# A three-stage mixer on one core: centred rows in place of normalized ones, paired folds and sums, attention state in column halves, and a new hand-written order

## The chip, the cores and the metric

The kernel runs on one core of a Trainium2 chip. The metric is the device time of the core in microseconds (us), as the median of several runs. A profiled execution gives the trace that the rows below come from. Engines: PE is TensorE's matmuls, PEld its weight loads, DVE is VectorE, ACT is ScalarE, POOL is GpSimd, SP is SyncE, which here issues DMAs.

## The reference

```python
def _attn_ref(q, k, v):                       # (2, 8, 768, 64) each, float32
    gamma = 1.0 - 2.0 ** (-5.0 - np.arange(H))
    for t in range(S):
        state = gamma * state + outer(k[:, :, t], v[:, :, t])
        y[:, :, t] = scale * (q[:, :, t] @ state)

def _moe_ref(x, w_ch1, w_ch2):                # x: (2, 768, 512), weights 512x2048, 2048x512 float64
    X = np.fft.fft(np.fft.fft(x, axis=1), axis=2)
    u = x + np.real(X)
    un = (u - mean(u)) / np.sqrt(var(u) + 1e-06)
    return u + np.maximum(un @ w_ch1, 0.0) @ w_ch2

def _moe2_ref(x, w_in, conv_w, w_out):        # weights 512x1024, 3x1024, 1024x512 float64
    h = np.maximum(x @ w_in, 0.0)
    conv_out = three-tap convolution of h along the sequence
    return (h * sigmoid(conv_out)) @ w_out
```

The three run one after the other. Data is float32, weights arrive as float64 and are turned into float32 on the chip.

## The kernel before, in words

Everything is a job, a short Python function that issues a few instructions. A string, ORDER, names the jobs one by one, and each engine gets its instructions in exactly that order; there is no scheduler. Each engine runs its own queue in order and waits at an instruction until its data and its buffers are there. A number such as 7 in a name is one of 12 chunks of 128 tokens, 6 for each of the two batches.

Attention. Lq, Lk, Lv load a chunk's tiles (256 KB each) through SP's queue, V scales v by the decay on POOL (L225), K and Q transpose k and q on PE (L231) with a copy by ACT (L232), S makes the scores of 8 heads in 64-row halves (L244, masked by DVE on L246), A adds the chunk to the running state (L256: per pair of heads one matmul of 128x128, of which only the two diagonal 64x64 blocks are used, copied by ACT on L260), O makes the output from state (L274) and scores (L277), and DVE scales it (L288).

Mixing. F folds a chunk's 512 features to sums and differences on POOL (L306 to L308), G folds again on DVE (L314 to L317, four instructions). After six chunks of a batch b, butterflies b0.0 to b0.9 combine the chunks (DVE, three of them on POOL: L337, L347, L348), t is the transform along the tokens (PE L369 to L373, copied by ACT on L374, L375), p the one along the features (L385 to L394), m and r add it to the residual stream u: m the first half of the tokens by DVE (L418, L419, two L411), r the other half, gathered in reverse by an indirect DMA (rev), by POOL (two L411).

First block. s takes mean and variance (L489, L490), dev the square root on ACT (L494), rec the reciprocal with one Newton step on DVE (L499 to L504, six small instructions for a group of three tiles), n normalizes a tile (L509, DVE), x transposes it (L531) and splits it in a high and a low part (ACT L535, DVE L536). U multiplies by a slice of the first weights, with ReLU on ACT (L560) and its low part on DVE (L561), D multiplies by the second and accumulates in PSUM, Z adds the sum to u (L572). Every product is three fp32r matmuls (high by high, high by low, low by high: L131 to L133). Batch 0 takes the 16 weight slices in three groups, batch 1 in one.

Weights. f fetches half a slice (512 KB), d decodes float64 to float32 on DVE (L465 to L469), e splits into high and low (ACT L459, then DVE or POOL L461).

Second block: y transposes, h the first product (tile hi), c, a, w the convolution, the gate and its split, P the last product (tile po) with a copy and the output DMA.

PSUM has eight banks, handed out in rotation. Batch 0 goes first through attention and mixing; its first block starts with U00.0 while batch 1 is still in attention and mixing, whose transform (t1) then stands between the first D jobs.

Of the kernel before, what the change touches and what calls it, by code (L numbers as in the profile page):

```python
# [16 lines left out]
P = 128  # L17
# [108 lines left out]
def mixer_kernel(ctx, tc, q, k, v, w_ch1, w_ch2, w_in, conv_w, w_out,  # L126
# [174 lines left out]
    def fold1(n):  # L301
# [78 lines left out]
    def dft_features(b, t):  # L380
        pq = pqt[b]

        def cosines(name, lo, rows):
# [3 lines left out]
            nc.tensor.matmul(g[0:rows, 129:257], pq[:, 1, lo:lo + rows], t2[:, 1, 0:P], start=True, stop=True)  # L387
# [6 lines left out]
        nc.tensor.matmul(qs[:, 129:257], pq[:, 3, sl], t2[:, 3, 0:P], start=True, stop=True)  # L394
        ny = cosines(f"ny{b}", HB, 1) if t == 0 else None
        mixes[b, t] = mix = fp.tile([P, 3, 258], F32, tag="h2", name=f"mix{b}{t}", bufs=H2)
        nc.scalar.copy(mix[:, 0, 0:257], qs[:, 0:257])
        products[b, t] = (pc, ny)

    def halves(b, t):  # L400
        w, e, dd = (mixes[b, t][:, i, :] for i in range(3))

        def low(x):
            return x.rearrange("p (j g) -> p j g", j=2)[:, :, 0:P]

        def high(x):
            return x[:, 1:257].rearrange("p (j g) -> p j g", j=2)[:, :, ::-1]

        def acc(eng, x, i, y):
            xv = x[:, t, i * 256:(i + 1) * 256].rearrange("p (g j) -> p j g", j=2)  # L410
            eng.tensor_tensor(xv, xv, y, op=ALU.add)  # L411

        return w, e, dd, low, high, acc

    def mixed(b, t):
        pc, ny = products[b, t]
        w, e, dd, low, high, acc = halves(b, t)
        nc.vector.tensor_tensor(dd[:, 0:257], pc[:, 0:257], w[:, 0:257], op=ALU.subtract)  # L418
        nc.vector.tensor_tensor(e[:, 0:257], pc[:, 0:257], w[:, 0:257], op=ALU.add)  # L419
        acc(nc.vector, u[b][0], 0, low(dd))  # L420
        acc(nc.vector, u[b][0], 1, high(e))
# [84 lines left out]
    def normalized(b, s, t):  # L506
# [64 lines left out]
    def residual(b, s, hi, t):  # L571
        nc.vector.tensor_tensor(u[b][s][:, t, :], u[b][s][:, t, :], accs[b, s, hi, t], op=ALU.add)  # L572
# [161 lines left out]
```

## Time and profile before

| what | value |
|---|---|
| median of 3 runs | 534.2 us (533.27 to 535.11) |
| profiled execution: its time, and the span of its trace | 531.92 us, 530.1 us |
| PE busy | 510.2 us (96%) |
| DVE busy | 337.7 us (64%) |
| ACT busy | 162.4 us (31%) |
| POOL busy | 87.6 us (17%) |
| mean granted TensorE clock | 0.997 |

Busy time counts the instructions of an engine that run, also while one stands in the pipeline behind another; the rest of the span is waiting. Each float32 matmul leaves two records in the trace, a transpose or an fp32r matmul one.

### The profile page before, as it was taken

How to read it: one execution, taken by the hardware profiler on the slowest of the kernel's cores; microseconds unless marked ns; L12 is line 12 of the kernel's file. 1: busy time of each engine (PE TensorE's matmuls, PEld its weight loads, DVE VectorE, ACT ScalarE, POOL GpSimd, SP SyncE). 2: the span in 40 equal slices, each digit the busy share in tenths (PEclk: the TensorE clock that was granted, in tenths of full speed). 3: DMA queues.
4: the chain of work that ended last, by engine and by line, in shares of the span. 5: the costliest groups of instructions: out<-in, count | busy, mean ns of one | idle time of the engine just before them, and what ended most of it. 6: DMA issues, size and time to landing. Idle time of an engine off the chain costs nothing.

```text
span 530.1 us, 7396 instructions
## 1 busy us (share of the span) xinstructions
PE 510.2 (96%) x2968; PEld 460.5 (87%) x2968; DVE 337.7 (64%) x593; ACT 162.4 (31%) x303; POOL 87.6 (17%) x98
## 2 busy tenths in 40 slices
PE   6998897998999999999999999999999999999997
PEld 5897787977998989889988998988999999988886
DVE  1578999999799877865221114887746675756511
ACT  3332344314322222121111112232255664445200
POOL 1545773450132201100000000120000000000000
PEclk9999999998999999999999999999999999999999
DMA  9999540213464043322000000344000000011111
GB/s 192 222 250 272 163 140 0 101 41 120 143 211 130 16 156 120 119 81 41 1 0 1 0 1 0 120 158 160 0 1 1 1 1 0 21 40 41 40 41 59
DMA packets 60807, 42.49 MB, mean 80 GB/s; under 512 B 42083, under 2 KB 54884, under 8 KB 60774
## 3 DMA queue, kind: packets, MB, share of 16 engines
q1 hardware_dynamic: 60294, 40.46, 27.1%
q0 software_dynamic: 480, 1.57, 1.0%
q8 instruction: 23, 0.38, 0.3%
q14 instruction: 10, 0.08, 0.0%
HBM read 37.30 MB, written 4.72 MB: 79 GB/s over the span
## 4 chain that ended last, share of the span: by engine, by line
PE 73%; DVE 12%; DMA 5%; issue 4%; POOL 4%; ACT 1%; SPq 0%; POOLq 0%; DVEq 0%; ACTq 0%
PE ac L133 7%; PE ac L132 7%; PE ac L131 7%; PE h L131 6%; PE h L133 6%; PE h L132 6%; PE po L132 4%; PE hi L133 4%; PE po L131 4%; PE hi L131 4%; PE hi L132 4%; PE po L133 4%; DMA xin<-in_v_dram 2%; DVE word L467 2%; PE px L277 2%
## 5 line engine op out<-in xcount | busy, mean ns | idle before, releaser
L561 DVE SCALAR_TENSOR_TENSOR h<-h,h 128x384 fp32r<-128x384 f32 x64 | 34.5, 552 | 76.8 <-ACT h L560 76.8
L131 PE MATMUL ac<-wt,h 128*128 128x512 f32 x192 | 76.6, 399 | 0.0
L133 PE MATMUL ac<-wt,h 128*128 128x512 f32 x192 | 76.2, 397 | 0.3 <-DVE h L561 0.3
L132 PE MATMUL ac<-wt,h 128*128 128x512 f32 x192 | 75.7, 394 | 0.0
L560 ACT ACTIVATE h<-h 128x384 fp32r<-128x384 f32 x64 | 30.8, 490 | 127.1 <-PE h L133 124.6
L461 POOL TENSOR_TENSOR wt<-word,wt 128x512 fp32r<-128x512 f32 x16 | 21.8, 1360 | 215.5 <-ACT wt L459 215.5
L459 ACT CAST wt<-word 128x512 fp32r<-128x512 f32 x48 | 29.5, 620 | 91.0 <-DVE word L469 88.5
L133 PEld LDWEIGHTS ac<-wt,h 128*128 128x128 f32 x192 | 36.0, 188 | 9.8 <-DVE h L561 1.5
L618 DVE SCALAR_TENSOR_TENSOR cv<-hb,cw,cv 128x768 f32<-128x768 f32 x32 | 32.5, 1018 | 15.5 <-ACT cv L616 14.8
L132 PEld LDWEIGHTS ac<-wt,h 128*128 128x128 f32 x192 | 36.1, 188 | 6.4
L131 PEld LDWEIGHTS ac<-wt,h 128*128 128x128 f32 x192 | 36.1, 188 | 6.2
L132 PE MATMUL po<-wt,g 128*128 128x512 f32 (+1 forms) x104 | 39.2, 377 | 0.0
L131 PE MATMUL po<-wt,g 128*128 128x512 f32 (+1 forms) x104 | 39.2, 377 | 0.0
L133 PE MATMUL po<-wt,g 128*128 128x512 f32 (+1 forms) x104 | 39.1, 376 | 0.0
L467 DVE SCALAR_TENSOR_TENSOR word<-raw,word 128x512 int32<-128x512 int32 x48 | 36.7, 764 | 1.6
L469 DVE SCALAR_TENSOR_TENSOR word<-raw,word 128x512 int32<-128x512 int32 x48 | 36.5, 760 | 1.6
L461 DVE TENSOR_TENSOR wt<-word,wt 128x512 fp32r<-128x512 f32 x32 | 24.0, 749 | 14.7 <-ACT wt L459 14.7
L647 DVE COPY ob<-po 128x512 f32<-128x512 f32 (+1 forms) x13 | 8.4, 648 | 28.3 <-PE po L133 28.3
L465 DVE TENSOR_SCALAR word<-raw 128x512 int32<-128x512 int32 x48 | 22.9, 478 | 3.4 <-POOL wt L461 2.6
L277 PE MATMUL px<-xin,work 128*128 128x64 f32 x192 | 23.8, 274 | 0.9 <-DVE work L246 0.9
L277 PEld LDWEIGHTS px<-xin,work 128*128 128x128 f32 x192 | 22.7, 192 | 1.8 <-DVE work L246 1.6
L133 PEld LDWEIGHTS po<-wt,g 128*128 128x128 f32 x104 | 19.6, 188 | 3.9
(176 smaller groups left out, 1170.4 us busy)
## 6 DMA issues: line engine op xcount, KB each, us to landing
raw<-in_moe_w_ch_dram SPq DMA_DIRECT2D x32, 512.0 KB, 3.7
raw<-in_moe_w_out_dram SPq DMA_DIRECT2D x8, 512.0 KB, 3.4
raw<-in_moe_w_in_dram SPq DMA_DIRECT2D x8, 512.0 KB, 3.4
xin<-in_q_dram SPq DMA_DIRECT2D x12, 256.0 KB, 4.6
xin<-in_k_dram SPq DMA_DIRECT2D x12, 256.0 KB, 5.1
xin<-in_v_dram SPq DMA_DIRECT2D x12, 256.0 KB, 5.0
out_dram<-ob SPq DMA_DIRECT2D x11, 256.0 KB, 2.0
xd<-states SPq DMA_DIRECT2D x6, 256.0 KB, 3.2
```

Of the source, the lines that this page charges most:

```text
L131: nc.tensor.matmul(o, ah, bh, start=start, stop=False)
L132: nc.tensor.matmul(o, ah, bl, start=False, stop=False)
L133: nc.tensor.matmul(o, al, bh, start=False, stop=stop)
L277: nc.tensor.matmul(px[:, h * D:(h + 1) * D], at[:, h, :], v_tile(n)[:, h, :], start=c == 0 and h == 0, stop=h == H - 1, skip_group_check=True)
L459: nc.scalar.copy(wt[:, 0, j], f32(word))
L461: eng.tensor_tensor(wt[:, 1, j], f32(word), f32(wt[:, 0, j]), op=ALU.subtract)
L465: nc.vector.tensor_scalar(word, raw[:, :, 1], 3, 0x3FFFFFF8, op0=ALU.logical_shift_left, op1=ALU.bitwise_and)
L467: nc.vector.scalar_tensor_tensor(word, raw[:, :, 1], -0x40000000, word, op0=ALU.bitwise_and, op1=ALU.bitwise_or)
L469: nc.vector.scalar_tensor_tensor(word, raw[:, :, 0], 29, word, op0=ALU.logical_shift_right, op1=ALU.bitwise_or)
L560: nc.scalar.activation(h2[:, 0], ps[:, :HB], AF.Relu)
L561: nc.vector.scalar_tensor_tensor(h2[:, 1], ps[:, :HB], 0.0, f32(h2[:, 0]), op0=ALU.max, op1=ALU.subtract)
L618: nc.vector.scalar_tensor_tensor(cv, hb[:, j:j + S], f32(cw[:, j * NF2 + f:j * NF2 + f + 1]), cv, op0=ALU.mult, op1=ALU.add)
```

## The change

- **Centred rows.** n only subtracts the mean; the division by the deviation is moved behind the second product, into Z, which multiplies the sum by 1/deviation while it adds it to u (ReLU lets a positive factor through). So x and U no longer need dev and rec, Z does. For 9 of 12 tiles the subtraction is an ACT instruction with the negated mean as bias, and s gets one small DVE instruction for that. The pools of the statistics are four deep in place of two.
- **Folds and mixed sums in pairs.** G is two DVE instructions of 2x128 in place of four; F is two POOL instructions, and two ACT instructions of one column. m is two instructions of 2x129 and one of 512 in place of two and two; r is one POOL instruction in place of two. Some matmuls of p get a 129th column.
- **State by heads in column halves.** A is, per head, one matmul with 64 weight columns and 64 moving columns, in place of one of 128x128 per pair of heads.
- **Work moved.** O's scaling of chunks 0, 6, 7 goes from DVE to ACT in 8 instructions of 64 columns each; V of chunk 5 from POOL to ACT in 8 also; F of chunk 4 and butterflies b0.2 and b1.2 from POOL to DVE. Five decoded words lie in PSUM banks. The identity is loaded from ACT's queue, Lv1 from POOL's.
- **A new job, warm:** three matmuls of 128x512 on zeros into a bank that nobody reads.
- **A new ORDER.** Its first line, of before and of the change, shows the start.

```diff
 ORDER = """
-Lq0 ident clear Q0 Lk0 K0 Lk1 K1 Lv0 masks V0 S0 A0 Lq1 Lk2 Lq2 Lv1 V1 Lk3 Lv3 V3 Q1 Lq3 O0 Lv5 F0 Q2 Lq4 S1 V5 G0 K3
+Lq0 clear Lv0 Lv3 ident masks V0 V3 Q0 Lk0 K0 A0 Lv1 S0 V1 Lq1 Lk1 K1 Lq2 Lk4 Lk2 Lv2 V2 Lk3 Lv4 Q1 Q2 Lq4 Lq3 f2 f0
...
+PX_ACT = (0, 6, 7)
+V_ACT = (5,)
+FOLD_DVE = (4,)
+FLY_DVE = ((0, 2), (1, 2))
+LOW_POOL = (0, 3, 6, 9, 12, 15, 18, 21, 24, 27, 30, 33, 36, 39, 40, 42)
+WORD_BANK = (2, 8, 22, 37, 38)
+CENTRE_ACT = ((0, 0, 0), (0, 0, 1), (0, 0, 2), (0, 1, 0), (1, 0, 1), (1, 0, 2), (1, 1, 0), (1, 1, 1), (1, 1, 2))
+WARM = (512, 512, 512)
...
+    def start_clock():
+        ps = bank("idle")
+        z = sbd[0].rearrange("p a e -> p (a e)")
+        for n in WARM:
+            nc.tensor.matmul(ps[:, 0:n], z[:, 0:P], z[:, 0:n], start=True, stop=True)
...
         for hp in range(NP):
-            nc.tensor.matmul(st[:, hp * P:(hp + 1) * P], pair(k_tile(n), hp), pair(v_tile(n), hp),
+            for j in range(2):
+                lo = hp * P + j * D
+                nc.tensor.matmul(st[j * D:(j + 1) * D, lo:lo + D], k_tile(n)[:, 2 * hp + j, :], v_tile(n)[:, 2 * hp + j, :],
...
-        nc.vector.tensor_tensor(o[:, 0:129], e[:, 0:129], e[:, 256:127:-1], op=ALU.add)
-        nc.vector.tensor_tensor(o[:, 129:256], od[:, 1:128], od[:, 255:128:-1], op=ALU.subtract)
-        nc.vector.tensor_tensor(o[:, 256:384], e[:, 0:128], e[:, 256:128:-1], op=ALU.subtract)
-        nc.vector.tensor_tensor(o[:, 384:512], od[:, 1:129], od[:, 255:127:-1], op=ALU.add)
+        o2 = o.rearrange("p (k n) -> p k n", k=4)
+        nc.vector.tensor_tensor(o2[:, 2:0:-1, :], eod2[:, :, 0:P], eod2[:, :, 256:P:-1], op=ALU.subtract)
+        nc.vector.tensor_tensor(o2[:, 0:4:3, :], two(0, 259), two(129, 257)[:, :, ::-1], op=ALU.add)
...
-        nc.vector.tensor_scalar(un, u[b][s][:, t, :], mv[:, t, 0:1], ve[:, 2, t:t + 1],
-                                op0=ALU.subtract, op1=ALU.mult)
+        if (b, s, t) in CENTRE_ACT:
+            nc.scalar.activation(un, u[b][s][:, t, :], AF.Identity, bias=ve[:, 4, t:t + 1])
+        else:
+            nc.vector.tensor_scalar(un, u[b][s][:, t, :], mv[:, t, 0:1], None, op0=ALU.subtract)
...
-        nc.vector.tensor_tensor(u[b][s][:, t, :], u[b][s][:, t, :], accs[b, s, hi, t], op=ALU.add)
+        nc.vector.scalar_tensor_tensor(u[b][s][:, t, :], accs[b, s, hi, t], norm[b, s][1][:, 2, t:t + 1], u[b][s][:, t, :],
+                                       op0=ALU.mult, op1=ALU.add)
```

Three places of the order follow, as the built programs have it. First PE's queue early in attention (pk, pq: transposes; px: O's matmuls; st: the state; idle: the bank of warm). Before, from K3 to O1:

```order
L231 MATMUL pk_192<-ident,xin_77 128x128 x4
L256 MATMUL st_129<-xin_80,xin_79 128x128 x4
L231 MATMUL pq_210<-ident,xin_80 128x128 x4
L274 MATMUL px_217<-states,work_82 128x128 x4
L277 MATMUL px_217<-xin_80,work_82 128x64 x8
```

With the change, from K2 to the second state update:

```order
L244 MATMUL pk_207<-ident,xin_77 128x128 x4
L289 MATMUL px_213<-states,work_82 128x128 x4
L292 MATMUL px_213<-xin_80,work_82 128x64 x8
L222 MATMUL idle<-states 128x512 x3
L271 MATMUL st_112<-xin_80,xin_79 64x64 x8
```

The state takes eight matmuls in place of four, and warm stands between O1 and it.

Second, ACT's queue ahead of batch 0's transform along the tokens (g is t's bank, pq its result). Before, the last rows ahead of t0.4's copies and those copies:

```order
L232 COPY work_83<-pq_576 128x512
L232 COPY work_83<-pk_610 128x512
L459 CAST wt_569<-word_459 128x512
L374 COPY pq_618<-g_619 1x6x64
L375 COPY pq_618<-g_619 1x1
```

With the change:

```order
L301 ACTIVATE u_72<-px_633,decay 128x64 x8
L301 ACTIVATE u_72<-px_661,decay 128x64 x8
L245 COPY work_82<-pq_682 128x512
L323 ACTIVATE eod<-u_72 128x1
L324 ACTIVATE eod<-eod 128x1
L396 COPY pq_696<-g_697 1x6x64
L397 COPY pq_696<-g_697 1x1
```

The scaling of O6 and O7, 16 instructions, and the single columns of F7 now stand ahead of the copies of t.

Third, what stands ahead of the first tile that x transposes. Before, on DVE (ve: the deviations; un: the normalized tile):

```order
L246 TENSOR_TENSOR work_83<-sc_824,mask 128x4x128
L499 TENSOR_SCALAR ve_713<-mv_712 128x3
L500 RECIPROCAL ve_713<-ve_713 128x3
L501 TENSOR_TENSOR ve_713<-ve_713 128x3
L502 TENSOR_TENSOR ve_713<-ve_713 128x3
L503 TENSOR_SCALAR ve_713<-ve_713 128x3
L504 TENSOR_TENSOR ve_713<-ve_713 128x3
L509 TENSOR_SCALAR un_849<-u_70,mv_712,ve_713 128x512
```

With the change, on ACT, between the copies of p:

```order
L419 COPY mix_768<-qs_765 128x258
L447 COPY mix_759<-ny_755 1x2x129
L448 COPY mix_759<-ny_755 1x2x129
L541 ACTIVATE un_781<-u_70,ve_776 128x512
L419 COPY mix_790<-qs_787 128x258
```

The tile un no longer stands behind the six small instructions, and it is on another engine.

## Rows read from the trace of the kernel before

**Rows 1.** Busy time of each engine in four stretches (start:end, length, busy us, records).

```profile
4.17:98.10 93.93, 84.59 (x751) 76.77 (x752) 73.96 (x139) 33.34 (x70) 49.58 (x59) 1.00 0.73 176
98.10:121.30 23.20, 20.49 (x111) 18.33 (x110) 22.88 (x42) 4.70 (x9) 11.21 (x11) 1.00 0.18 58
121.30:160.00 38.70, 38.70 (x216) 34.86 (x217) 33.74 (x58) 13.73 (x29) 8.58 (x8) 0.96 0.54 170
160.00:526.00 366.00, 365.72 (x1891) 329.97 (x1890) 206.65 (x355) 109.31 (x194) 17.08 (x15) 1.00 0.15 48
```

**Rows 2.** Whom PE waited for, whole span: us in total, times, longest.

```profile
PE pq L231 <- DMA ident<-in_c_ident_dram: 4.2, 1, 4.2
PE g L369 <- issue: 2.3, 1, 2.3
PE tr L531 <- DVE un L509: 2.2, 2, 1.7
PE g L369 <- DVE fold L351: 1.9, 1, 1.9
PE pq L231 <- DMA xin<-in_q_dram: 1.3, 1, 1.3
...
PE st L256 <- POOL xin L225: 0.9, 1, 0.9
...
PE h L132 <- DVE un01l L536: 0.8, 1, 0.8
```

**Rows 3.** Stretches of 2 us around t1's start; the granted clock is the third last.

```profile
120.00:122.00 2.00, 0.73 (x8) 0.61 (x9) 1.93 (x4) 0.00 (x0) 0.00 (x0) 0.92 0.00 0
122.00:124.00 2.00, 2.00 (x10) 1.31 (x9) 1.28 (x3) 1.05 (x3) 0.00 (x0) 0.50 0.01 1
124.00:126.00 2.00, 2.00 (x15) 2.00 (x15) 1.93 (x4) 1.37 (x4) 0.00 (x0) 0.72 0.80 239
```

**Rows 4.** Timeline, the first centred tile's chain of before.

```profile
84.22 1.28 ACT L494 ACT_TABLE_LOAD   x1
...
87.92 1.00 DVE L509 TENSOR_SCALAR un<-u,mv,ve 128x512 f32<-128x512 f32 x2
...
89.07 0.63 PE L531 MATMUL tr<-ident,un 128*128 128x128 f32 x4 [1.73 <-DVE un L509]
```

**Rows 5.** Groups of DVE instructions, whole span: busy us, mean ns of one.

```profile
L314 DVE TENSOR_TENSOR fold<-eod 128x129 f32<-128x129 f32 x12 | 6.6, 551 | 3.6 <-POOL eod L307 3.5
...
L315 DVE TENSOR_TENSOR fold<-eod 128x127 f32<-128x127 f32 x12 | 5.3, 439 | 0.0
L317 DVE TENSOR_TENSOR fold<-eod 128x128 f32<-128x128 f32 x12 | 4.4, 367 | 0.0
...
L316 DVE TENSOR_TENSOR fold<-eod 128x128 f32<-128x128 f32 x12 | 3.4, 280 | 0.0
...
L418 DVE TENSOR_TENSOR mix<-pc,mix 128x257 f32<-128x257 f32 x6 | 2.5, 410 | 0.0
```

**Rows 6.** Timeline, attention: start, length, instruction.

```profile
14.89 0.97 PEld L244 LDWEIGHTS sc<-work 64*128 64x128 f32 x16 [0.17 <-issue]
...
16.47 1.06 PE L256 MATMUL st<-xin,xin 128*128 128x128 f32 x8
...
31.70 1.87 PEld L277 LDWEIGHTS px<-xin,work 128*128 128x128 f32 x16
```

**Rows 7.** Timeline, the start: first scores, and a load's issue on SP's queue.

```profile
8.02 2.08 PE L244 MATMUL sc<-work 64*128 64x128 f32 x16
...
8.23 1.07 SPq L191 DMA_DIRECT2D xin<-in_v_dram  x1
```

**Rows 8.** Groups of ACT instructions, whole span.

```profile
L374 ACT COPY pq<-g 128x384 f32<-128x384 f32 x8 | 7.1, 892 | 3.2 <-PE g L373 3.2
...
L375 ACT COPY pq<-g 128x1 f32<-128x1 f32 x8 | 1.9, 233 | 0.0
...
L630 ACT CAST g<-cv 128x128 fp32r<-128x128 f32 x4 | 1.2, 299 | 0.0
```

More of the change, by code (lines that the diff above doesn't have):

```diff
@@ L206, in clear @@
     def clear():
+        nc.vector.memset(sbd[0], 0.0)
+        nc.gpsimd.memset(sbd[1], 0.0)
         nc.vector.memset(eps, EPS)
-        for i in range(2):
-            nc.gpsimd.memset(sbd[i], 0.0)
+    def start_clock():
[3 more added lines that the diff above has]
+            nc.tensor.matmul(ps[:, 0:n], z[:, 0:P], z[:, 0:n], start=True, stop=True)
     xdram = {}
@@ L386, in cosines @@
             nc.tensor.matmul(g[0:rows, 0:129], pq[0:1, 4, lo:lo + rows], alt, start=False, stop=True)
-            nc.tensor.matmul(g[0:rows, 129:257], pq[:, 1, lo:lo + rows], t2[:, 1, 0:P], start=True, stop=True)
+            nc.tensor.matmul(g[0:rows, 129:258], pq[:, 1, lo:lo + rows], t2[:, 1, :], start=True, stop=True)
             return g
@@ L398, in dft_features @@
+        nc.scalar.copy(mix[:, 0:258], qs[:, 0:258])
         products[b, t] = (pc, ny)
     def halves(b, t):
[L401 to L411, printed above, removed]
@@ L413, in halves, with runs, two_runs, features @@
-        return w, e, dd, low, high, acc
+        m = mixes[b, t]
+        def runs(lo, n):
+            return m[:, lo:lo + 2 * n].rearrange("p (j g) -> p j g", j=2)[:, :, 0:P + 1]
+        return runs(0, P + 1), runs(258, P + 2), runs(518, P + 1)[:, :, ::-1], m[:, 258:778].rearrange("p (i s) -> p i s", i=2)
+    def two_runs(x):
+        return x[:, 0:258].rearrange("p (j g) -> p j g", j=2)
+    def features(x):
+        return x.rearrange("p (i g j) -> p i j g", i=2, j=2)
     def mixed(b, t):
@@ L416, in mixed @@
         pc, ny = products[b, t]
[L417 to L421, printed above, removed]
+        w, dd, e, both = halves(b, t)
+        nc.vector.tensor_tensor(dd, two_runs(pc), w, op=ALU.subtract)
+        nc.vector.tensor_tensor(e, two_runs(pc), w, op=ALU.add)
@@ L422, in mixed @@
+        x = features(u[b][0][:, t, :])
+        nc.vector.tensor_tensor(x, x, both.rearrange("p i (j g) -> p i j g", j=2)[:, :, :, 0:P], op=ALU.add)
         if t == 0:
-            nc.scalar.copy(e[0:1, 0:257], ny[0:1, 0:257])
-            nc.scalar.copy(dd[0:1, 0:257], ny[0:1, 0:257])
+            nc.scalar.copy(e[0:1], two_runs(ny)[0:1])
+            nc.scalar.copy(dd[0:1], two_runs(ny)[0:1])
     def mixed_back(b, t):
-        w, e, dd, low, high, acc = halves(b, t)
+        both = halves(b, t)[3]
@@ L428, in mixed_back @@
         eng = nc.vector if (b, t) in BACK_DVE else nc.gpsimd
-        acc(eng, u[b][1], 0, low(e))
-        acc(eng, u[b][1], 1, high(dd))
+        x = features(u[b][1][:, t, :])[:, ::-1]
+        eng.tensor_tensor(x, x, both[:, :, 1:259].rearrange("p i (j g) -> p i j g", j=2)[:, :, :, P - 1::-1], op=ALU.add)
     chunks = {}
@@ L450, in decode @@
         i, j = divmod(h, 2)
-        words[h] = word = fp.tile([P, 512], I32, tag="word", name=f"word{i}{j}", bufs=2)
+        if h in WORD_BANK:
+            words[h] = word = psum.tile([P, 512], I32, tag="ps", name=f"word{i}{j}")
+        else:
+            words[h] = word = fp.tile([P, 512], I32, tag="word", name=f"word{i}{j}", bufs=2)
         to_float32(word, raws[h])
@@ L680, in mixer_kernel @@
                 jobs[f"s{b}{s}.{t}"] = later(moments, b, s, t)
-                jobs[f"n{b}{s}.{t}"] = later(normalized, b, s, t)
+                jobs[f"n{b}{s}.{t}"] = later(centred, b, s, t)
                 jobs[f"x{b}{s}.{t}"] = later(norm_transposed, b, s, t)
```

98 lines of the change are left out of this document (52 added, 46 removed).

## The prediction

> **What bounds the kernel now.** I read the four stretches first [rows 1]. From 121.3 us to 526 PE is busy 404.4 of 404.7 us, with fp32r products back to back: nothing that DVE, ACT or POOL saves there shortens anything, since PE has no wait to give up. What can be won lies ahead of that, where two stretches wait. From PE's first matmul at 4.17 to U00.0 at 98.1 PE is busy 84.59 of 93.93 us, so 9.3 us are waits; from 98.1 to 121.3 it is busy 20.49 of 23.20, so 2.7 are. The other engine to look at is DVE: 74.0 of 93.9 in the first of these, but 22.88 of 23.20 in the second. There DVE is full, and PE waits for it.
>
> Second, whom PE waits for [rows 2]. The first wait (4.2 us, for the identity and the first q) is the head, which stays, as the first q sets it too. Of the rest, four are named by the change: 2.2 us in two waits of x's transposes for un, 2.3 us of t0's first matmul (its butterflies are the last of a DVE and POOL chain, although the row names no engine), 1.9 us of t1's first matmul for the last butterfly of batch 1, and 0.9 and 0.8 us for V and for the low part of a tile. 1.3 us is for a load.
>
> Third, the clock [rows 3]. After the 1.9 us wait, which ends at 121.27, the granted clock is 0.92, 0.50 and 0.72 in three stretches of 2 us, so near 1.2 GHz in the middle one, and 1.00 again after. Lost are (0.08 + 0.50 + 0.28) times 2 us, 1.7 us, within busy time that no wait shows. So t1's wait costs 3.6 us, not 1.9.
>
> All that could be won from waits and clock is then 9.3 + 2.7 + 1.7 = 13.7 us, 2.6% of the time.
>
> **The change part by part.** The sum is made against the profiled execution, 531.92 us; the median of the runs, 534.2, is 2.3 above it, and I add that at the end.
>
> *Centred rows.* Before, x's first transpose waits 1.73 us for un, which DVE ends after ACT has loaded the table for the square root (1.28 us, from 84.22) and after the six small instructions of rec [rows 4]. Now un needs only the mean; it stands on ACT among the copies of p, before the table is loaded at all. Both waits for un can go: **-2.2 us**. Bounds 0 and -2.2: 0 if something else is then late at that place, such as the scores of chunk 10, which DVE masks there. Z now needs dev and rec, but Z comes four D jobs after U00.0, and stays one DVE instruction on the same two tiles; I price that at nothing. The cover is those D jobs; without it Z would pay the old 2.2 us.
>
> *Pairs on DVE.* The four instructions of G take 551 + 439 + 367 + 280 ns on average, 1.64 us; where POOL is quiet each takes what the L316 row shows, 0.28, so 1.12 [rows 5]. The two that replace them have 256 columns each, like the 257 of L418, 0.41: 0.82 us. A chunk saves 0.3 to 0.8 us, twelve chunks 3.6 to 9.8; I take 6, as half of the L314 mean is waiting on POOL's side. The three scalings and four subtractions that go to ACT are set against F4, b0.2, b1.2 and a memset that come to DVE, and the merged mixed sums are a small gain on top. So DVE does 6 to 8 us less before t1 out of 97 [rows 1]. This isn't time by itself; it is what shortens the waits for DVE: t0's 2.3 us, t1's 1.9 with its 1.7 of clock, and the two small ones.
>  - t0: the butterflies of batch 0 also wait for POOL, whose part of that chain stays but for b0.2. I take half, **-1.1** (bounds 0, -2.3).
>  - t1: between U00.0 and t1 the same six U and three D jobs stand as before, so PE's cover is the same, and DVE has the last of the four-instruction folds and POOL's three folds out of that stretch. The lead wanted is 1.9 us of 22.9. I take all, **-3.6** (bounds 0, -3.6).
>  - V10 and the low part: half of 1.7, **-0.8**.
>
> *State in column halves.* Before, eight records of a state update take about 1 us: each is held by a weight load of 128 columns, about 0.12 us. With 64 columns there are 16 records. Two rows bound them [rows 6]. The output matmuls (L277) move 64 columns on weights of 128 and pass 16 records in 1.87: +0.8 to +0.9 us for each of ten updates, +8.5 in all. The score matmuls, in alternating 64-row halves, pass 16 records of 128 columns in 0.97, half the pace of the undivided ones, so halves run side by side there; if column halves do the same with half the columns, 16 take 0.5, -0.5 each, -4.9 in all. Half of the columns to load and half to move, one after the other, is 16 times 0.055, 0.88: **-0.9** over ten. I take that, being between.
>
> *Warm.* Three float32 matmuls of 512 columns. A state update before moves 4 times 128 columns in about 1 us [rows 6], so each costs that: 2.9 us of PE. Nothing hides it at its place, for PE has hardly a wait there; but some of the waits after it, 1.3 us for a q tile among them, are for loads that come no later for it. I take half, **+1.3** (bounds 0, +2.9). It comes too late for the start, where the first scores take 2.08 us [rows 7] against about 1 later [rows 6].
>
> *The start.* K0's load now stands behind q, two v, the mask and the decay on SP's queue, where it stood behind q and the identity; loads follow each other at about 1.1 us [rows 7], so K0 is 2 to 3 us later. V0, S0 and A0 needed the decay and v anyway, which come earlier now. **+0.5** (0 to +2.5).
>
> *ACT ahead of t0.* The scaling of O7 is now eight ACT instructions of 64 columns: between 233 ns for one column and 299 for 128 [rows 8], 0.25 each, so 2.1 us, and two single columns of F7 another 0.5. They stand in ACT's queue right before the first of t0's five pairs of copies (0.89 + 0.23 us a pair). PE's t jobs are slower than a pair by some tenths and p begins with what is copied first, which catches up part of 2.6: **+1.0** (0 to +2.6).
>
> *At nothing:* Z by deviation, the columns 129, words in PSUM, the identity's queue, r in one instruction. They are behind a full PE or on engines with room (ACT 33 of 94 us, POOL 50 of 94 in the first stretch [rows 1]).
>
> Sum: -2.2 - 1.1 - 3.6 - 0.8 - 0.9 + 1.3 + 0.5 + 1.0 = -5.8. 531.92 - 5.8 = 526.1, and with the 2.3 between the profiled execution and the median, **528.4 us**, 1.1% faster.
>
> **The rivals.**
> 1. *Column halves at the price of the L277 rows.* Eight matmuls held by their loads cost +8.5 in place of -0.9: -5.8 + 9.4 = +3.6, **537.8 us**, slower. Against it: the weights are half as wide here. For it: where a queue goes from undivided to row halves, the score's first load shows 0.17 us of idle with nothing waited for [rows 6]; two such changes for each of ten updates would add up to 3.4 us, 541.2 with both. The Trainium skill ("TensorEngine Tiling (Array Packing)", Key Properties) says that a change of tiling mode drains TensorE; no run here yet shows it for column halves. It decides from 1.6 us for an update, against 1.0 before: there the other terms are used up.
> 2. *Waits move, they don't go.* The loads set the pace until about 50 us, DVE's place at t1 is taken by two decoded halves and butterfly b1.2, and PE waits for those. Then -2.2, -1.1 and -3.6 shrink to a third (-2.3), and the additions stay: -2.3 - 0.4 - 0.9 + 2.8 = -0.8, **533.4 us**, no difference. For it speaks that DVE is 99% busy before t1 and the first long DVE chains are unchanged.
> 3. *More than forecast.* Halves side by side (-4.9 in place of -0.9) and all waits named gone (-1.2 - 0.8 more), warm hidden (-1.3): -5.8 - 7.3 = -13.1, **521.1 us**.
>
> **How the numbers follow.** A measurement of this kernel can hardly tell 0.3%, 1.6 us, from no change. Forecast (524 to 531.5): 0.55. Rival 3 (518 to 524): 0.15. Rival 2 (within 1.6 us of 534.2): 0.13. Rival 1 and other losses, such as a start later by the full 2.5 us with warm unhidden: 0.17. So faster 0.70, same 0.13, slower 0.17. The range goes from near rival 3's own time, 520, to 535.5, just over rival 2; it leaves out the deepest part of rival 3 and most of rival 1, together below 2 in 10.
>
> **What would show it.** U00.0 starts near 94 us in place of 98.1, with no wait of tr for un. The first matmul of t1 waits less than 0.5 us and the granted clock stays at 1.00 there. A state update's 16 records take 0.8 to 1.0 us; 1.6 or more is rival 1, 0.5 rival 3. G takes near 0.8 us on DVE. After t1 PE is as full as before, and the stretch from t1 to the end is as long. The forecast is wrong if state updates are slow, if U00.0 starts at 98 or later, or if the new order puts a wait of PE behind 121 us, where there was none: there any wait costs its full length.

## The result, and the profile after

The changed kernel takes 528.83 us (median of 4 runs, 528.11 to 530.10), the kernel before beside it 534.65 (533.27 to 536.80): a ratio of 0.989, 95% interval 0.9851 to 0.9929. It is 1.1% faster. The profiled execution took 528.11 us, with a span of 526.3 against 530.1.

First the stretches of the changed kernel that answer to [rows 1]: up to U00.0, from there to t1's first matmul, the next 39 us, the rest. Behind them stand four stretches of 2 us around U00.0, and a stretch that comes up later; the granted clock is the third last number.

```profile
4.42:97.75 93.33, 83.69 (x838) 73.51 (x838) 66.60 (x120) 45.41 (x129) 48.17 (x48) 0.98 0.74 168
97.75:119.37 21.62, 21.58 (x107) 19.94 (x108) 18.48 (x33) 5.22 (x12) 4.42 (x4) 0.92 0.36 116
119.37:158.10 38.73, 38.73 (x222) 34.70 (x222) 32.87 (x60) 13.28 (x29) 6.81 (x6) 1.00 0.43 136
158.10:525.00 366.90, 364.66 (x1890) 330.06 (x1888) 205.72 (x352) 112.05 (x198) 18.39 (x14) 1.00 0.16 50
...
94.00:96.00 2.00, 0.89 (x4) 0.89 (x5) 1.86 (x7) 1.06 (x2) 0.35 (x1) 0.60 0.00 0
96.00:98.00 2.00, 1.32 (x7) 0.92 (x5) 1.13 (x3) 1.47 (x3) 2.00 (x3) 0.50 0.76 254
98.00:100.00 2.00, 1.96 (x6) 1.56 (x7) 2.00 (x5) 0.41 (x3) 0.30 (x1) 0.50 0.56 184
100.00:102.00 2.00, 2.00 (x10) 2.00 (x9) 1.16 (x4) 0.07 (x1) 0.76 (x1) 0.70 1.03 386
...
20.00:26.00 6.00, 6.00 (x60) 3.82 (x61) 4.74 (x8) 3.03 (x9) 1.71 (x2) 1.00 1.06 262
```

Second, whom PE waits for over the whole span; this answers to [rows 2].

```profile
PE pq L244 <- DMA xin<-in_q_dram: 4.4, 1, 4.4
PE sc L257 <- ACT work L245: 3.3, 4, 1.2
PE pk L244 <- DMA xin<-in_k_dram: 2.8, 1, 2.8
PE tr L564 <- ACT un L541: 2.0, 1, 2.0
PE h L136 <- ACT un00h L568: 0.7, 1, 0.7
PE st L271 <- ACT states L275: 0.4, 1, 0.4
```

Third, rows of the timeline, in order of time: warm, a state update, t0's start, ACT and PE ahead of U00.0, and the work around t1's start.

```profile
8.30 1.11 PE L244 MATMUL pk<-ident,xin 128*128 128x128 f32 x4 [2.79 <-DMA xin<-in_k_dram]
...
19.82 2.79 PE L222 MATMUL idle<-states 128*128 128x512 f32 x6
...
22.54 0.55 PEld L271 LDWEIGHTS st<-xin,xin 128*64 128x64 f32 x16 [0.76 <-issue]
22.54 0.69 PE L271 MATMUL st<-xin,xin 128*64 128x64 f32 x16
...
59.92 1.75 ACT L301 ACTIVATE u<-px,decay 128x64 f32<-128x64 f32 x8 [0.94 <-PE px L292]
60.25 0.27 PE L391 MATMUL g<-tabs,fold 128*1 128x65 f32 x2
...
92.38 1.28 ACT L524 ACT_TABLE_LOAD   x1
93.67 0.30 ACT L524 ACTIVATE ve<-mv,eps 128x3 f32<-128x3 f32 x1
93.87 0.56 ACT L568 CAST un01h<-tr 128x512 fp32r<-128x512 f32 x1
94.34 0.72 ACT L541 ACTIVATE un<-u,ve 128x512 f32<-128x512 f32 x1
95.11 1.97 PE L564 MATMUL tr<-ident,un 128*128 128x128 f32 x8 [1.97 <-ACT un L541]
97.75 0.69 PE L136 MATMUL h<-un00h,wt 128*128 128x384 f32 x1 [0.68 <-ACT un00h L568]
...
109.26 1.29 POOL L369 TENSOR_TENSOR fold<-fold,fold 128x512 f32<-128x512 f32 x1 [6.73 <-DVE fold L361]
...
117.29 0.69 DVE L373 TENSOR_TENSOR fold<-fold 128x512 f32<-128x512 f32 x1
119.37 0.33 PE L391 MATMUL g<-tabs,fold 128*128 128x65 f32 x2
```

What to see. t0 and t1 start without a wait, where 2.3 and 1.9 us stood before [rows 2]; t1's last butterfly ends at 117.98, 1.4 us early, where it was 1.9 us late. A state update passes its 16 records in 0.69 us, where eight took 1.06 [rows 6]. But the first matmul of U00.0 stands at 97.75, hardly ahead of 98.1. The wait for un is still there: 2.0 us, now for ACT, and 0.7 behind it. Tile n00.1, the centring of the first block's second tile, stands in ACT's queue behind two things of the other half of the tokens: its square root (dev01), whose table takes 1.28 us to load, and the split of its tile x01.0 (un01h). And the clock that was lost at t1 before [rows 3] is lost here. Counted in PE's busy time alone, since a low clock costs nothing while PE waits anyway, the four stretches lose 0.40 x 0.89 + 0.50 x 1.32 + 0.50 x 1.96 + 0.30 x 2.00, 2.6 us, against 1.6 by the same count from [rows 3].

Up to U00.0 the waits as a whole did not shrink: PE waits 9.6 us of the first stretch, where it was 9.3 [rows 1]. Two kinds grew. Scores wait 3.3 us in four places for ACT's copies of transposes, where it was 0.7 in one, and K's load costs 2.8 in place of 0.8. ACT is busy 45.4 us there in place of 33.3; whether that is what holds up the scores was not tried.

By stretch, the 3.8 us between the two spans are: 0.25 lost in the head, 0.6 won up to U00.0, 1.6 from there to t1, 1.9 behind t1's start, of which 1.7 is the clock that fell there before. The 2.2 us of the last stretch in which PE is not busy are the tail behind its last matmul, which ends near 522.9.

### The profile page after: what moved, and what is told of

The parts are those of the page before. It is cut to its first block, busy times and chain, and to the rows that moved or that the text cites. A ratio compares the mean times of both kernels' runs of the same rounds, so it can differ in the third digit from the quotient of the medians.

```text
span 526.3 us, 7589 instructions
## 1 busy us (share of the span) xinstructions
PE 508.7 (97%) x3054; PEld 458.2 (87%) x3054; DVE 324.2 (62%) x565; ACT 177.2 (34%) x368; POOL 78.5 (15%) x75
## 4 chain that ended last, share of the span: by engine, by line
PE 76%; DVE 6%; issue 6%; POOL 5%; ACT 3%; DMA 2%; SPq 1%; POOLq 0%
PE h L138 7%; PE h L136 7%; PE h L137 7%; PE ac L138 7%; PE ac L137 6%; PE ac L136 6%; PE hi L138 4%; PE hi L137 4%; PE hi L136 4%; PE po L136 4%; PE po L138 4%; PE po L137 4%; PE px L292 3%; PE sc L257 2%; PE tr L564 2%
## 5 line engine op out<-in xcount | busy, mean ns | idle before, releaser
L488 POOL TENSOR_TENSOR wt<-word,wt 128x512 fp32r<-128x512 f32 x16 | 21.2, 1323 | 224.5 <-ACT wt L486 214.1
L496 DVE SCALAR_TENSOR_TENSOR word<-raw,word 128x512 int32<-128x512 int32 x48 | 37.4, 779 | 1.6
L494 DVE SCALAR_TENSOR_TENSOR word<-raw,word 128x512 int32<-128x512 int32 x48 | 34.2, 712 | 1.6
L488 DVE TENSOR_TENSOR wt<-word,wt 128x512 fp32r<-128x512 f32 x32 | 22.0, 689 | 13.7 <-ACT wt L486 13.7
L492 DVE TENSOR_SCALAR word<-raw 128x512 int32<-128x512 int32 x48 | 24.3, 506 | 3.7 <-POOL wt L488 2.6
L259 DVE TENSOR_TENSOR work<-sc,mask 128x512 f32<-128x512 f32 x24 | 15.4, 684 | 17.0 <-PE sc L257 16.9
L136 PE MATMUL h<-un00h,wt 128*128 128x384 f32 x64 | 22.4, 350 | 0.7 <-ACT un00h L568 0.7
```

Of the source, the lines that this page charges most:

```text
L136: nc.tensor.matmul(o, ah, bh, start=start, stop=False)
L488: eng.tensor_tensor(wt[:, 1, j], f32(word), f32(wt[:, 0, j]), op=ALU.subtract)
L492: nc.vector.tensor_scalar(word, raw[:, :, 1], 3, 0x3FFFFFF8, op0=ALU.logical_shift_left, op1=ALU.bitwise_and)
L494: nc.vector.scalar_tensor_tensor(word, raw[:, :, 1], -0x40000000, word, op0=ALU.bitwise_and, op1=ALU.bitwise_or)
L496: nc.vector.scalar_tensor_tensor(word, raw[:, :, 0], 29, word, op0=ALU.logical_shift_right, op1=ALU.bitwise_or)
```

## The experiments

Each kernel was timed in five rounds against the kernel before; "ratio" is to that kernel. Unless said otherwise an experiment starts from the changed kernel. They ran in three groups, and medians are best compared within a group: the first four, the next four, the last four.

**The changed kernel once more (a0_again).** No edit.

> The changed kernel once more, beside the others of this call on the same chip: ratio to before 0.989 as on record, about 528.8 us. It gives the ground that the others are measured from, and a second profile: if the 2.0 us wait for the centred tile and the clock of 0.5 after it are the work of the order and not of one execution, they stand there again.

527.90 us, ratio 0.9888 (0.9859 to 0.9918), with the same 2.0 us wait of tr, the same fall of the clock there, and t1 at 119.09. This is what the others of its group stand against.

**The second root later (e1_root_later).** dev01 and rec01 moved behind U00.0's tiles:

```diff
-... F11 s01.1 dev01 rec01 O10 x01.0 n00.1 ... U01.1 f7 d7 e7 t1.0 dev00 rec00 t1.2 ...
+... F11 s01.1 O10 x01.0 n00.1 ... U01.1 f7 d7 e7 t1.0 dev00 rec00 dev01 rec01 t1.2 ...
```

> dev01 and rec01 (ACT's table load, 1.28 us, and root, 0.30) move from ahead of the centred tile n00.1 to behind rec00; nothing else. Theory A (the wait that centring was to remove came back because dev01 stands ahead of n00.1 in ACT's queue): un starts where x01.0's transposes free its buffer, at about 93.2 in place of 94.34, so the wait of 1.97 us falls to 0.8, the clock falls for a shorter time, and the kernel is 1 to 4 us faster than the changed one (525 to 528). Theory B (U00.0 is held by the DVE and PE work of chunks 10 and 11): U00.0 stays at 97.7 and the time within 0.5 us of the changed kernel.

528.41 us, ratio 0.9889 (0.9863 to 0.9915): no gain, where theory A had 1 to 4 us. At its place the edit did a part of what was meant: tr waits 1.3 us in place of 2.0, the clock stays at 1.00, U00.0 starts at 96.77 and t1 at 117.27, 1.8 us sooner than in a0_again.

```profile
94.95 1.09 PE L564 MATMUL tr<-ident,un 128*128 128x128 f32 x8 [1.30 <-ACT un L541]
```

So the root accounts for 0.7 of the 2.0 us. In the 1.3 that stay, n00.1 still stands behind x01.0, the other half's tile: ACT splits that at 93.69 and centres n00.1 at 94.17. Then PE waits 1.5 us for a weight slice (L488) near 130 and 0.5 us for DVE's h, where there was no wait.

**The first block's tiles first (e7_block_first).** On top of that, n00.1 ahead of the other half's tiles:

```diff
-x00.0 n01.0 s01.2 ... s01.1 O10 x01.0 n00.1 x00.1 x00.2 n01.1 n01.2 ... b1.5 x01.1 ...
+x00.0 n00.1 s01.2 ... s01.1 O10 x00.1 x00.2 n01.0 n01.1 ... b1.5 x01.0 n01.2 x01.1 ...
```

> As e1, and the three tiles of U00.0 are centred and transposed before any tile of the other half (n00.1 takes the place of n01.0, x01.0 stands behind U00.1). Theory A: no wait of tr for un, the granted clock stays at 1.00, U00.0 starts 3 us earlier and runs at full rate: 4 to 6 us faster than the changed kernel (523 to 525). Theory B: U00.0 starts at 97 or later, time within 1 us of the changed kernel. A new wait of U01 for the later tiles would give back part.

527.44 us, ratio 0.9877 (0.9849 to 0.9905): still no difference that these runs can tell. Ahead of U00.0 no wait of tr is left (one of 1.0 us for a tile of the other half ends at 107.92). U00.0 starts at 94.66 and t1 at 116.75, 2.3 us sooner than in a0_again, and most of it goes at 130 us again. Two rows of the timeline, on DVE and PE:

```profile
122.88 0.18 DVE L530 RECIPROCAL ve<-ve 128x3 f32<-128x3 f32 x1 [1.61 <-ACT ve L524]
...
130.05 0.45 PE L136 MATMUL h<-un01h,wt 128*128 128x384 f32 x1 [1.54 <-DVE wt L488]
```

The roots now stand in ACT's queue behind the first of t1's copies; DVE's reciprocal waits 1.61 us for them, and behind it in DVE's queue stand the decoded weights for which PE comes 7 us later. A job moved out of one queue's way had been put into another's.

**The state as it was (e2_state_pairs).**

```diff
-            for j in range(2):
-                lo = hp * P + j * D
-                nc.tensor.matmul(st[j * D:(j + 1) * D, lo:lo + D], k_tile(n)[:, 2 * hp + j, :], v_tile(n)[:, 2 * hp + j, :], ...
+            nc.tensor.matmul(st[:, hp * P:(hp + 1) * P], pair(k_tile(n), hp), pair(v_tile(n), hp), ...
```

> The changed kernel with the state update of before (four matmuls of 128x128). Theory A (halves run side by side, 0.55 us of loads for 16 records against 0.97 for 8, on PE's path): ten updates cost 4 us more, 532 to 533 us. Theory C (PE waits for loads or scores where the update stands, so its 4 us were hidden): within 1 us of the changed kernel, and the waits of PE before 90 us shrink by as much.

530.45 us (530.18 to 531.63), ratio 0.9933 (0.9907 to 0.9959), 2.5 us above the changed kernel in the same group, of whose six runs one (530.62) reaches into this range: more than theory C had, less than theory A. U00.0 starts at 99.20 and t1 at 122.08. In this order the column halves are worth 2.5 us, of the 4 that PE's records give.

**Both roots early (e8_roots_early).** From e7, dev00 and dev01 ahead of D00.1, so ahead of t1's copies in ACT's queue:

```diff
-b1.8 b1.9 e10 D00.1 U01.0 D00.2 U01.1 f7 d7 e7 t1.0 dev00 rec00 dev01 rec01 t1.2 ...
+b1.8 b1.9 e10 dev00 dev01 D00.1 U01.0 D00.2 U01.1 f7 d7 e7 t1.0 rec00 rec01 t1.2 ...
```

> As e7, and both roots (dev00, dev01) stand in ACT's queue ahead of D00.1, where ACT is a quarter busy, in place of behind the first copies of t1, where DVE's rec00 waited 1.61 us for them in e7. Theory A (e7's gain of 2.3 us at t1 was given back because DVE's weights were late behind that wait): the 1.54 us wait of PE at 130 us goes, and the kernel takes 526 us or less, 1.5 us under e7. Theory D (DVE has no room left there whatever ACT does): time as e7, 527.4.

525.48 us (525.04 to 525.95), ratio 0.9851 (0.9820 to 0.9882). Three rows of its waits, then the stretch from U00.0 to t1:

```profile
PE tr L564 <- DVE un L543: 1.0, 1, 1.0
PE h L136 <- ACT un00h L568: 0.7, 1, 0.7
PE h L137 <- DVE un00l L569: 0.4, 1, 0.4
```

```profile
93.52:115.61 22.09, 20.73 (x112) 18.95 (x113) 21.45 (x35) 8.14 (x17) 5.78 (x5) 1.00 0.40 131
```

The 1.0 us is for a tile of the other half and ends at 106.77, behind U00.0; the other two stand at its start. U00.0 starts at 93.52, 4.2 us ahead of the changed kernel's (0.4 of that is there at t0 already, which starts at 59.82), the clock is 1.00 throughout, and the wait at 130 us is gone. So the 2.0 us wait and its clock are traced to places in ACT's queue: 0.7 us to the root (e1), the rest to the other half's tile (e7). With the first block's tiles ahead of both, and the roots ahead of what waits behind them, the forecast's "U00.0 starts near 94 us" comes true, in another order.

**Column halves alone (e3_before_halves).** The kernel before with the new state update and nothing else.

> The kernel before with the state update in column halves alone. If ten updates of 0.69 in place of 1.06 us lie on PE's path in that order too: 2.5 to 4 us faster than before (530 to 532). If PE only arrives earlier at its waits for DVE (t0, un, t1), which the shorter updates do not move: within 1 us of before.

533.35 us, ratio 1.0003 (0.9973 to 1.0033): no difference. Its update passes 16 records at the new pace, and PE waits the longer for it: in its profile, which is of its slowest run, t0's wait is 4.3 us, and t1's is still 1.9. That profile also has more time at a low clock than the one of before (mean 0.981 against 0.997), so its waits alone don't price the edit. In the order of before, what PE saves in attention doesn't reach the end, or less than 1.5 us of it (the lower end of the interval).

**Without warm (e4_no_warm).** The job dropped from the order.

> The changed kernel without the job warm (three matmuls of 512 columns, 2.8 us of PE at 19.8 us). If half is hidden, as predicted: 1.3 us faster than the changed kernel. If it is all on the path: 2.8 us faster. If the scores and copies behind it wait for loads and ACT anyway: no difference; and if the clock falls in a wait that warm filled, slower, with a granted clock under 1.00 between 20 and 30 us.

528.55 us (527.09 to 531.33), ratio 0.9906 (0.9871 to 0.9940): no difference. The profiled execution was the slowest of its runs; a stretch of it:

```profile
20.00:26.00 6.00, 3.44 (x35) 2.89 (x30) 4.06 (x8) 2.35 (x7) 1.71 (x2) 0.66 1.13 273
```

PE is busy 3.44 of the 6 us where it was full with warm, since it now waits for a q tile, and the clock there is 0.66, not 1.00. Warm fills a wait that is there anyway. Two of the six runs, this one and one of 530.26, have a mean clock of 0.987 and 0.986; the other four, like the changed kernel, 0.992 or more.

**Four folds again (e5_four_folds).** G back in four instructions, in the new order.

```diff
-        nc.vector.tensor_tensor(o2[:, 2:0:-1, :], eod2[:, :, 0:P], eod2[:, :, 256:P:-1], op=ALU.subtract)
-        nc.vector.tensor_tensor(o2[:, 0:4:3, :], two(0, 259), two(129, 257)[:, :, ::-1], op=ALU.add)
+        nc.vector.tensor_tensor(o[:, 0:129], e[:, 0:129], e[:, 256:127:-1], op=ALU.add)
+        ... (129:256, 256:384 and 384:512 likewise)
```

> The changed kernel with the second fold in the four instructions of before. If the pairs are what freed DVE ahead of t1: about 0.3 to 0.8 us more of DVE for each of twelve chunks, t1 late by 1 us or more with a wait of PE for the last butterfly, 2 to 4 us slower. If t1's wait went because of the order and the moved butterfly: within 1 us of the changed kernel.

528.78 us, ratio 0.9910 (0.9876 to 0.9944): no difference. DVE spends 15.1 us on G in place of 11.4, and t1's first matmul, at 118.80, waits for nothing: the last butterfly ends at 117.40, again 1.4 us early. So the pairs on DVE, on which the forecast in part rested t1's gain, don't carry it.

**Butterfly b1.2 back on POOL (e9_fly_pool).** `FLY_DVE = ((0, 2),)`.

> The changed kernel, only that butterfly b1.2 of batch 1 goes back from DVE to POOL, where it was before. Theory A: t1's wait is gone because POOL works little beside DVE's last butterflies (4.4 us of POOL between U00.0 and t1, against 11.2 before), so that DVE's run at 0.69 us each and not 1.66. Then with b1.2 on POOL the chain before t1 is longer by 1 to 2 us, t1's first matmul waits again for 0.5 to 2 us, some clock goes with it, and the time is 529 to 531.5. Theory B: the order alone took the wait away, with lead to spare: no wait at t1, and the time within 1 us of the changed kernel's 528.

528.74 us, ratio 0.9897 (0.9870 to 0.9924): theory B. The last butterfly and t1's first matmul:

```profile
118.53 0.69 DVE L373 TENSOR_TENSOR fold<-fold 128x512 f32<-128x512 f32 x1
...
119.57 0.33 PE L391 MATMUL g<-tabs,fold 128*128 128x65 f32 x2
```

The chain ends 1.2 us later, at 119.22, and still 0.35 us ahead of PE. The move to DVE buys lead that nothing needs here.

**The new code in the old order (e10_old_order).** The order of before, without warm; all other edits stay.

> The changed kernel's code in the order of before (without warm, which that order doesn't have). Theory A: the edits shorten what DVE and PE do, and the order only arranges it: 528 to 531, with the transposes' wait for un gone, since un there stands ahead of the second square root. Theory B: the gain is made by the order, which puts V8, the roots and the butterflies where they no longer hold PE up: 532 to 535, with the waits at t0 and t1 still there.

536.25 us (531.99 to 539.07), ratio 1.0033 (1.0006 to 1.0060): slower than before, by a little more than both theories allowed; theory B is the nearer. Its waits:

```profile
PE px L292 <- DVE work L259: 4.1, 3, 2.0
PE sc L257 <- ACT work L245: 3.3, 3, 1.9
PE g L391 <- issue: 2.1, 1, 2.1
PE g L391 <- DVE fold L373: 1.7, 1, 1.7
PE h L137 <- DVE un01l L569: 1.3, 1, 1.3
```

The waits at t0 (2.1) and t1 (1.7) are there as before, and there is none of tr for un. So the centring takes away its wait by itself; the waits at t0 and t1 are the order's. New are 4.1 us of waits for masked scores (0.9 in before's profile), and the clock is at 0.66 from 44 to 48 us and at 0.50 from 48 to 52, where it was 1.00 before. It falls again behind the waits at t0, at 94.74 for masked scores, and at t1: 8.5 us of lost clock up to 140 us, against 1.7 in before's profile, which is more than the 5.3 us between the two spans (535.4 and 530.1). The reverse, the code of before in the new order, was not timed. Ahead of t1, on POOL and DVE (rows of one engine each):

```profile
119.58 1.74 POOL L369 TENSOR_TENSOR fold<-fold,fold 128x512 f32<-128x512 f32 x1 [5.61 <-DVE fold L361]
121.39 1.61 POOL L370 TENSOR_TENSOR fold<-fold,fold 128x512 f32<-128x512 f32 x1
...
120.19 1.67 DVE L364 TENSOR_TENSOR fold<-fold 128x512 f32<-128x512 f32 x1
121.89 1.66 DVE L366 SCALAR_TENSOR_TENSOR fold<-fold,fold 128x512 f32<-128x512 f32 x1
```

POOL's two instructions of b1.8 run beside DVE's butterflies, and two of these take 1.67 and 1.66 us, while the others there take 0.69.

**K0's load earlier (e11_k_first).** From e8:

```diff
-Lq0 clear Lv0 Lv3 ident masks V0 V3 Q0 Lk0 K0 A0 Lv1 S0 V1 ...
+Lq0 clear Lk0 ident Lv0 masks Lv3 V0 V3 Q0 K0 S0 A0 Lv1 V1 ...
```

> The version with both roots early (525.5 us), only that K0's load stands third in the start and V0, V3, Q0, K0, S0 and A0 follow in that order. The forecast's theory, that the later load of K0 costs 0.5 to 2.5 us: the 2.8 us wait for K shrinks to about 1, the first scores come 1 to 2 us earlier, and of that 0 to 2 us reach the end: 523.5 to 525.5. The rival, that the stretch up to 60 us is paced by the later loads and by DVE: the waits move on to a later load, and the time is within 1 us of 525.5.

524.79 us (524.17 to 525.36), ratio 0.9825 (0.9796 to 0.9854): the fastest version here, 0.7 us under e8, which stood in another group; the two intervals overlap, so they are not told apart. The start did change:

```profile
5.51 1.11 PE L244 MATMUL pk<-ident,xin 128*128 128x128 f32 x4
7.30 2.08 PE L257 MATMUL sc<-work 64*128 64x128 f32 x16 [0.67 <-ACT work L245]
```

The first scores start at 7.30, 3 us ahead of the changed kernel's 10.39. At warm 0.9 of that is left (18.97 against 19.82), and t0 starts at 60.2 in both. The rival holds: what is won at the start is gone before t0, part of it in new short waits for loads.

**O6 and O7 scaled on DVE (e6_px_dve).** `PX_ACT = (0,)`.

> The changed kernel, only that the scalings of O6 and O7 go from ACT back to DVE. The forecast's theory, that these 16 instructions hold up ACT's copies of t0 by about 1 us: p begins earlier and the time is about 1 us less, 527. The rival, that ACT has room there and DVE has not: t0's first matmul waits again for 0.5 to 1.5 us, as DVE has 1.5 to 2 us more to do ahead of the butterflies, and the time is 528.5 to 530.

536.91 us (535.83 to 540.36), ratio 1.0069 (1.0044 to 1.0094): 8 us slower than the changed kernel, and neither theory had it. ACT's queue and PE behind t0, then the clock:

```profile
66.67 0.20 ACT L323 ACTIVATE eod<-u 128x1 f32<-128x1 f32 x1 [5.14 <-DVE u L303]
...
67.65 0.81 ACT L396 COPY pq<-g 1x384 f32<-1x384 f32 x1
...
69.21 0.49 PE L407 MATMUL pc<-tabs,pq 128*128 128x129 f32 x2 [1.60 <-ACT pq L397]
...
71.47 0.68 PE L415 MATMUL qs<-tabs,pq 128*128 128x129 f32 x2 [0.93 <-ACT pq L397]
```

```profile
70.00:72.00 2.00, 1.07 (x7) 0.83 (x6) 0.79 (x3) 1.41 (x6) 1.84 (x2) 0.91 0.03 8
72.00:74.00 2.00, 2.00 (x9) 0.53 (x8) 0.94 (x3) 0.37 (x1) 1.39 (x3) 0.50 0.45 131
```

The single column of fold F7, one instruction of 0.20 us that this change puts on ACT, needs the scaled output of O7. With that scaling on DVE, behind two decoded half slices, the column waits 5.14 us, and all copies of t0 wait behind it: they start at 67.65, not at 63.13. PE loses 2.5 us of waits for p, 0.4 more for un, and 5.1 us of clock (7.8 us of its busy time up to 110 us, against 2.7 in the changed kernel, by stretches of 0.25 us): 8.0 of the 8.2 us between the spans.

## Why the prediction was right, step by step

The total was right: 1.1% faster, 528.83 us against 528.4. That it came so close is luck, in two ways. The terms forecast 5.8 us between the two profiled executions, and 3.8 were measured (531.92 to 528.11). The forecast then added 2.3 us from the profiled execution to the median, and for the changed kernel that step is 0.7. The second error hides most of the first: the kernel before had a mean clock of 0.997 in its profiled execution and 0.986 to 0.997 in the 23 runs of the last group, the changed kernel 0.992 to 0.994 in its four. And among the terms errors cancel too.

- *Centred rows, -2.2.* This step failed. "It stands on ACT among the copies of p, before the table is loaded at all" holds for the first tile, not for the second, n00.1, which stands behind dev01's root and the split of the other half's x01.0. The wait of 2.2 us came back as 2.0 and 0.7, the bound of 0 that the text gave, but for another reason than it named. With it came 2.6 us of lost clock that no term had. e10 shows that the edit by itself removes the wait; e1 and e7 show that this order gave it back, 0.7 us by the root and the rest by the tile.
- *t0's wait, -1.1.* All of 2.3 went; t0 starts 1.4 us sooner. The forecast's half was too small, and e10, where 2.1 us are back with the same code, shows that the code without the order doesn't do it.
- *t1, -3.6.* The wait and its clock went as forecast. The reason didn't hold: neither the pairs (e5) nor b1.2 (e9) is needed, although DVE has even more room than forecast (66.60 + 18.48 us up to t1 in place of 73.96 + 22.88, 11.8 less, not 6 to 8), and in the old order the pairs don't help (e10, 1.7 us). What the order does is read from the rows: in the old one POOL's part of b1.8 overlaps DVE's last butterflies (e10); in the new one it starts at 109.26, ahead of them, and each of them takes 0.69. That this one move is the whole of it was not tried apart from the order.
- *V10 and a low part, -0.8.* The two waits that take their places are 0.4 and 0.7 us, against 0.9 and 0.8; the 0.7 is the one that the first term has already.
- *State in column halves, -0.9.* The mechanism was right and the size was off. The update of 16 records takes 0.69 us, between the forecast's 0.88 and rival 3's 0.5, some 0.4 less than before for each of ten; undoing it costs 2.5 us. The forecast's 0.055 us for a record was also less than half of its own 0.12 for a load of 128 columns; with half, 0.06, the same sum leaves no gain. Rival 1 (1.6 us or more) is refuted. The weight loads stand idle for 0.76 us ahead of the update in the row above, with nothing waited for, and 0.16 at the next, but PE itself does not (6.00 busy of 6.00 us), and e2's undivided loads stand idle there too, 0.24 and 0.27. The Trainium skill ("TensorEngine Tiling (Array Packing)", Key Properties) says that a change of tiling mode drains TensorE; no run here sets such a drain apart, and if there is one, it doesn't eat the gain.
- *Warm, +1.3.* It takes 2.79 us of PE as forecast and costs nothing at the end (e4): it is hidden in the wait for a q tile.
- *Start, +0.5.* K0 waits 2.8 us, yet having it 3 us sooner doesn't move t0 (e11). The term is 0, within what 0.7 us leaves open.
- *ACT ahead of t0, +1.0.* The eight instructions took 1.75 us, not 2.1, and p waits for nothing, so it cost 0. What the step left out is that the scaling has to be there: F7's columns follow it in the same queue, and e6 pays 8 us without it.
- *Behind t1.* PE is as full as before there. The forecast's warning, that any wait behind 121 us costs its full length, came true in e1 and e7, not in the changed kernel.

Of the signs that the forecast named, t1's two and the stretch behind t1 came as it said. U00.0 at 97.75 is just short of the 98 that was to refute it, tr still waits for un, G takes 0.95 us and not 0.8, and an update 0.69 and not 0.8 to 1.0.

Rival 2 said that waits move. One of its three did, the wait for un, and it cost its clock as well; that is the 3 us which e8 gets back. The longer waits for K and for the scores' copies, 4.6 us more than before, are of its kind too. Between the two profiles PE waits 2.3 us less, works 2.5 us less with warm included, and loses 1.0 us more to the clock. The state, t0, warm and ACT came out better than forecast; the centring, and waits that no term had, worse.

## What to carry to other kernels

In queues that run in order, price a moved instruction by what stands ahead of it and behind it in its new queue, not by its own length: here 0.20 us on ACT decides over 8 us, and the place of one root and one tile of the other half over 3. When a wait of PE goes, follow the same job to the queues it now stands in, and look for the next wait further on: e1 and e7 gave at 130 us back what they had gained at 95. Time an edit in the order that it is meant for, and that order with each edit undone: column halves are worth 2.5 us in the new order and nothing that the runs can tell in the old.

## What the runs showed of the hardware

- A wait of PE may cost more in clock than its length. Around the waits of 2.0 and 0.7 us at 95 to 97.75 the granted clock was 0.50 in two stretches of 2 us, and 2.6 us of PE's busy time were lost; behind e6's 1.6 and 0.9 it was 0.50 until 81.5. The waits of 0.7 and 0.4 us at U00.0 in e8, and of 1.3, 0.7 and 0.4 in e1, left it at 1.00. The length alone doesn't decide it: t0's wait of 2.3 us before [rows 2] left the clock at 1.00, and the one of 2.1 us at the same place in e10 was followed by 0.50 from 66 to 69.
- Float32 matmuls in two column halves with 64 columns of weights ran 16 records in 0.69 us, where eight undivided ones of 128 took 1.06 [rows 6].
- DVE's butterflies with both inputs in SBUF took 0.69 us alone and 1.66 to 1.67 beside POOL's butterflies, and POOL's went from 1.29 to 1.61 and 1.74 (e10). The Trainium skill ("SBUF — State Buffer", SBUF: two separate sides) says that the two share a port pair which one of them holds for a whole instruction; these rows agree in that both get slower, and the size was not worked out.
